# Three layers on one core: the experts' second product on 512 columns at once, and an output written in whole rows

## The chip, the core and the metric

The kernel runs on one core of one Trainium2 chip. The metric is the device time of one execution in microseconds (us), lower is better. Engines named here: PE (TensorE, matrix products), DVE (VectorE), ACT (ScalarE), POOL (GpSimd), and SP (SyncE), whose queue issues all transfers of this kernel. Matrix results land in PSUM, eight banks of 512 fp32 columns on 128 partitions; PSUM has to be copied to SBUF by DVE or ACT before a transfer can take it to HBM.

## What is computed

The reference chains three layers over 2304 tokens (4 batches of 576) of width 512: attention in a window (four heads) or a dilated window (four heads), a feed-forward layer `g = h - tanh(h)` with `h = x @ w_in` and `g @ w_out`, and a soft mixture of 8 experts with 4 slots each. The change lies at the end of the third:

```
logits = x @ phi                                   # 2304 x 32 slots
slot_input = softmax_over_tokens(logits).T @ x     # 32 x 512
for e in range(8):                                 # 4 slots each
    h = np.maximum(slot_input[e] @ w1[e], 0.0)     # 512 -> 1024
    slot_out[e] = h @ w2[e]                        # 1024 -> 512
c = softmax_over_slots(logits)                     # 2304 x 32
return c @ slot_out                                # 2304 x 512
```

## The kernel before

The program is written as one order of instructions per engine; nothing is reordered by a scheduler. Attention, the two weight matrices of the feed-forward layer, its tokens in chunks and the statistics of the logits fill the time up to about 440 us; there the slots' inputs are made. Nothing of this is touched.

Then follow the experts. Their weights are 32 tiles of 1 MB (`w1t`, `w2t`, two of each kind per expert, rows of 1024 fp32 in a tile), loaded by `load_experts` (L672, L676) into a ring of 21 equal buffers (`unit`) as these come free; in the trace they are named `ex`, their source `in_moe_w_dram`. `expert_up` makes the hidden layer of an expert, `expert_relu` turns it into columns in `hT`, which holds zeros but for the expert's own 4 of 32 slots, so that all experts can add into one result of 32 slots.

`expert_down(e, y, cols)` (L706 to L713) is the second product: 8 matmuls that take 32 columns of `hT` as weights and stream 256 columns of `w2t`. Four of them at a time stand on the four column strips of the PE array, so `y` has four partial sums on its 128 partitions. The columns are treated in two halves, each with its own PSUM tile (`ys`). The constant `DOWN` (L32) sets the order of experts and halves: experts 0 to 6 of half 0, experts 0 to 2 of half 1, expert 7 of half 0, the rest of half 1.

`combine(y, a)` is a generator that finishes half `a`: DVE copies `y` to SBUF (L1015); a product with `sum3` (L1018) adds the four strips and gives the result three times; ACT rounds it to a shorter fp32 form (L1019) and DVE puts the rounding error into the third copy (L1020), together `sS` (trace: `fin`); then nine pieces of output follow. Each is two matmuls `o` of 128 tokens by 256 columns (L1031) with the softmax weights `cT` or `cR`, one copy out of PSUM, by DVE for even pieces (L1038) and ACT for odd ones (L1036), and a write. A token's number is 4i + r in its batch; one tile `cT[:, b, r]` has 128 tokens of equal r. A piece holds r and r + 1 for 128 values of i, and its write (L1044) sends, for each token, 256 columns: 1 KB. The last piece holds the 64 left-over tokens of each batch and is written by four transfers of 64 KB (L1042). The pieces of half 0 are made two at a time between the experts of half 1.

Of the kernel before, what the change touches and what calls it, by code (L numbers as in the profile page):

```python
# [8 lines left out]
F32 = mybir.dt.float32  # L9
# [19 lines left out]
MASKPE = 2  # L29
PO = (2, 3, 0, 1)  # L30
ENGS = {'qk': 'AAAAVAAVVVAA', 'pt': 'AAA', 'hi': 'AAA', 'rem': 'VVA', 'wh': 'AV', 'wt': 'AA', 'wq': 'VA', 'wp': 'A', 'g': 'AAAA'}
DOWN = [(0, e) for e in range(7)] + [(1, e) for e in range(3)] + [(0, 7)] + [(1, e) for e in range(3, 8)]  # L32
WARM = 5
NWARM = 4
WAT = 0.29
# [25 lines left out]
def moe_kernel(ctx: ExitStack, tc: tile.TileContext, q, k, v, w_in, w_out, phi, w1, w2, out):  # L61
    nc = tc.nc
    B, H, S, D = q.shape
    DM, DFF = w_in.shape
    NS = phi.shape[1]
    NE, _, FE = w1.shape
# [8 lines left out]
    ps_h = ctx.enter_context(tc.tile_pool(name="ps_h", bufs=2, space=PSUM))  # L75
    ps_l = ctx.enter_context(tc.tile_pool(name="ps_l", bufs=1, space=PSUM))
    ps_m = ctx.enter_context(tc.tile_pool(name="ps_m", bufs=5, space=PSUM))

    def mm(shape):
        return ps_m.tile(shape, F32, tag="mm", name="mm")  # L80
# [15 lines left out]
    def copy(eng, out, in_):  # L96

        (nc.scalar.copy if eng == "A" else nc.vector.tensor_copy)(out=out, in_=in_)  # L98
# [7 lines left out]
    def unit(name, shape, dt=F32):  # L106
        return sb.tile(shape, dt, tag="unit", bufs=UNITS, name=name)

    def cpart(*dims):
        o = moff[0]  # L110
        moff[0] += size(dims)
        return view(mem[:, o:o + size(dims)], dims)

    class Ring:
# [5 lines left out]
        def next(self):  # L120
            self.n += 1
            return self.places[(self.n - 1) % len(self.places)]
# [30 lines left out]
    t_sb = cpart(512)  # L153
# [473 lines left out]
    halves = [slice(0, 256), slice(256, 512)]  # L627
# [19 lines left out]
    w1t, w2t, h1, hT = {}, {}, {}, []  # L647
# [55 lines left out]
            op0=ALU.max,  # L703
        )

    def expert_down(e, y, cols):  # L706
        for n in range(8):
            j, i = divmod(n, 2)
            qd = n % 4
            nc.tensor.matmul(  # L710
                y[32 * qd:32 * qd + 32, :], lhsT=hT[0][:, e, i, j, :], rhs=w2t[e, j // 2][:, j % 2, i, cols],
                start=(e == 0 and n < 4), stop=(e == NE - 1 and n >= 4), tile_position=(0, 32 * qd),
            )  # L713

# [57 lines left out]
    with tc.manual_schedule():  # L772
        conv_tiles()
        consts()
        steps = []
# [4 lines left out]
        for b, (t0, dt) in enumerate((ATT0, ATT1)):  # L780
            for i in range(NU):
                t = t0 + dt * i
# [16 lines left out]
        for e in range(NFT):  # L799
            t, dt = (WO1[0] + WO1[1] * e, WO1[1]) if e < KA else (WO2[0] + WO2[1] * (e - KA), WO2[1])  # L800
# [6 lines left out]
            t, dt = WI[0] + WI[1] * e, WI[1]  # L807
# [11 lines left out]
        for ft in range(NFT):  # L819
            t = HT[0] + HT[1] * ft  # L820
# [23 lines left out]
        for ch in range(1, 4):  # L844
            xh, xl = xhi[ch], xlo[ch]
            if ch == 3:
# [6 lines left out]
                t = unit("gr", [128, 3, 512])  # L853
# [4 lines left out]
            for s in range(NFT // 2):  # L858
                a, b = 2 * s, 2 * s + 1
# [40 lines left out]
        for s in range(NFT // 2):  # L900
            a = 2 * s
            ps = ps_h.tile([128, 512], F32, tag="h", name="h").rearrange("p (i t) -> p i t", i=2)
# [57 lines left out]
        for a, copy in enumerate((nc.scalar.copy, nc.vector.tensor_copy)):  # L960
            ps = mm([128, 2, 128])
# [7 lines left out]
        ps = mm([128, 512])  # L969
        for c in range(4):  # L970
            for fq in range(4):
                nc.tensor.matmul(
                    ps[32 * fq:32 * fq + 32, :], lhsT=tT[:, c, 32 * fq:32 * fq + 32], rhs=wo[fq][:, c, :],
                    start=(c == 0), stop=(c == 3), tile_position=(0, 32 * fq),
# [7 lines left out]
        for a, copy in enumerate((nc.scalar.copy, nc.vector.tensor_copy)):  # L982
            ps = mm([128, 2, 32])
# [20 lines left out]
        cT, cR, sS = fins  # L1004


        ov = out.rearrange("(b i r) d -> b i r d", b=B, r=4)
        ofl = out.rearrange("(b t) d -> b t d", b=B)
        sum3 = stack.rearrange("p j s -> p (j s)")[:, 0:96]

        def combine(y, a):

            cols = slice(256 * a, 256 * a + 256)
            ys = t_sb[:, cols]
            nc.vector.tensor_copy(out=ys, in_=y)  # L1015
            yield
            ps = mm([96, 256])
            nc.tensor.matmul(ps, lhsT=sum3, rhs=ys, start=True, stop=True)  # L1018
            nc.scalar.copy(out=sS[:, cols], in_=ps)  # L1019
            nc.vector.tensor_tensor(  # L1020
                out=sS[64:96, cols], in0=ps[64:96], in1=sS[64:96, cols].bitcast(F32), op=ALU.subtract
            )
            yield
            units = [(b, r) for b in range(B) for r in (0, 2)] + [(None, 0)]
            o = None
            for t, (b, r) in enumerate(units):
                pool = (ps_h, "h") if t % 3 == 0 else (ps_m, "mm")
                ps = pool[0].tile([128, 2, 256], F32, tag=pool[1], name="o")
                for x in range(2):
                    lhsT = cR[:, 2 * x:2 * x + 2].rearrange("p b i r -> p (b i r)") if b is None else cT[:, b, r + x]  # L1030
                    nc.tensor.matmul(ps[:, x], lhsT=lhsT, rhs=sS[:, cols], start=True, stop=True)  # L1031
                if t % 4 == 0:
                    o = unit("o", [128, 4, 2, 256])
                od = o[:, t % 4]
                if t % 2:
                    nc.scalar.copy(out=od, in_=ps)  # L1036
                else:
                    nc.vector.tensor_copy(out=od, in_=ps)  # L1038
                if b is None:
                    for n in range(B):  # L1040
                        x, h = divmod(n, 2)
                        nc.sync.dma_start(out=ofl[n, 512:576, cols], in_=od[64 * h:64 * h + 64, x])  # L1042
                else:
                    nc.sync.dma_start(out=ov[b, 0:128, r:r + 2, cols], in_=od)  # L1044
                yield


        ys = [ps_l.tile([128, 256], F32, tag="lg", name="y"), mm([128, 256])]
        halves2 = [combine(y, a) for a, y in enumerate(ys)]
        for a, e in DOWN:  # L1050
            expert_down(e, ys[a], halves[a])
            if a and DOWN.index((a, e)) > DOWN.index((0, NE - 1)):
                for _ in range(2):
                    next(halves2[0], None)
            if (a, e) == (0, NE - 1):
                next(halves2[0])
        for steps in halves2:
            for _ in steps:
                pass


# [28 lines left out]
```

## Time and profile before

| | before |
|---|---|
| time, median of 3 runs | 506.72 us (506.23 to 509.2) |
| the profiled execution | 506.77 us |
| its span, first to last instruction | 505.0 us |
| PE busy | 467.6 us, 93% of the span |
| DVE, ACT, POOL busy | 226.1, 233.6, 83.5 us |
| mean granted clock of PE | 0.973 of full |
| moved by DMA | 81.16 MB, 159 GB/s over the span |
| writes of the output | 16 of 256 KB and 8 of 64 KB |

The busy shares are means over stages with different limits, so they do not say what the last 40 us are bound by. The rows further down are read for that: the chain of waits tells which step the end hung on, a timeline tells what an engine did and what ended its idle time, and a table of stretches shows busy time, granted clock and DMA rate side by side. A group of matmuls in a timeline shows the time from the first start to the last end, with the drain of the last.

### The profile page before, as it was taken

To read this page: it belongs to the slowest core of one execution; us is meant where nothing else is said; L and a number is where in the kernel's file an instruction comes from. 1 tells how busy PE (TensorE), PEld (TensorE's weight loads), DVE (VectorE), ACT (ScalarE), POOL (GpSimd) and SP (SyncE) were. 2 spreads that over 40 slices of the span, in tenths; PEclk is the share of its full clock that TensorE was granted. 3 is DMA by queue.
4 is the path that set the end of the run, shared out by engine and by line. 5 is a ranking of instruction groups with operands and counts; after the bars stand their busy time and mean duration, and the time that the engine had idled before them with its cause. 6 is when DMAs were issued, how large, how long until landed. Compare 5 with 4: busy or idle time off the path is not lost.

```text
span 505.0 us, 11720 instructions
## 1 busy us (share of the span) xinstructions
PE 467.6 (93%) x4741; PEld 353.9 (70%) x4741; DVE 226.1 (45%) x560; ACT 233.6 (46%) x761; POOL 83.5 (17%) x99
## 2 busy tenths in 40 slices
PE   6879778999999999999999899999999999999872
PEld 5656556877777868888786778877677879645442
DVE  1669988945754435433242453432312231232032
ACT  3647636575655464675364556543223323213022
POOL 3263455432341010211011011100000000010000
PEclk9959988999999999999999999999999999999995
DMA  8989899644145602212310100219500279899946
GB/s 213 209 213 291 290 310 307 195 121 119 28 144 115 101 2 51 73 49 47 86 38 1 37 1 3 85 58 412 198 1 1 84 278 393 323 392 407 375 156 220
DMA packets 65029, 81.16 MB, mean 161 GB/s; under 512 B 35792, under 2 KB 44240, under 8 KB 64976
## 3 DMA queue, kind: packets, MB, share of 16 engines
q1 hardware_dynamic: 64976, 80.42, 50.8%
q8 instruction: 37, 0.61, 0.5%
q14 instruction: 16, 0.13, 0.1%
HBM read 71.50 MB, written 8.91 MB: 159 GB/s over the span
## 4 chain that ended last, share of the span: by engine, by line
PE 77%; DVE 8%; DMA 4%; ACT 4%; issue 4%; POOL 1%; SPq 0%; POOLq 0%; ACTq 0%; DVEq 0%
PE h L502 13%; PE h L503 12%; PE h L504 12%; PE mm L536 5%; PE mm L304 5%; PE lg L517 4%; PE mm L358 4%; DMA ex<-in_moe_w_dram 3%; PE mm L337 3%; PE mm L634 3%; PE mm L266 3%; PE h L685 2%; ACT mem L316 2%; DVE cva L442 1%; PE o L1031 1%
## 5 line engine op out<-in xcount | busy, mean ns | idle before, releaser
L502 PE MATMUL h<-xhi,whi 128*128 128x512 f32 x256 | 107.0, 418 | 0.0
L504 PE MATMUL h<-xhi,wlo 128*128 128x512 f32 x256 | 100.9, 394 | 0.0
L503 PE MATMUL h<-xlo,whi 128*128 128x512 f32 x256 | 100.8, 394 | 0.0
L508 ACT ACTIVATE mem<-h 128x512 f32<-128x512 f32 x56 | 33.4, 596 | 83.7 <-PE h L504 83.7
L511 DVE TENSOR_TENSOR mem<-h,mem 128x512 f32<-128x512 f32 x56 | 38.6, 689 | 73.1 <-ACT mem L508 72.8
L328 POOL TENSOR_TENSOR mem<-mem 128x320 f32<-128x320 f32 (+1 forms) x48 | 34.5, 718 | 188.5 <-DVE mem L327 126.0
L502 PEld LDWEIGHTS h<-xhi,whi 128*128 128x128 f32 x256 | 48.6, 190 | 13.2 <-issue 5.0
L504 PEld LDWEIGHTS h<-xhi,wlo 128*128 128x128 f32 x256 | 48.4, 189 | 10.8
L503 PEld LDWEIGHTS h<-xlo,whi 128*128 128x128 f32 x256 | 48.9, 191 | 8.9 <-DVE xlo L390 0.7
L98 ACT COPY g<-mm 128x512 f32<-128x512 f32 x72 | 40.2, 597 | 11.9 <-PE mm L549 4.8
L316 ACT ACTIVATE mem<-mm,mem 128x80 f32<-128x80 f32 (+1 forms) x84 | 26.8, 330 | 30.8 <-DVE mem L313 30.8
L316 ACT ACTIVATE mem<-mem 128x80 f32<-128x80 f32 (+1 forms) x84 | 29.9, 357 | 16.5 <-DVE mem L313 14.4
L304 PE MATMUL mm<-qk 64*64 64x96 f32 (+2 forms) x672 | 35.0, 250 | 1.9 <-DVE qk L98 1.9
L304 PEld LDWEIGHTS mm<-qk 64*64 64x64 f32 (+1 forms) x672 | 28.1, 135 | 10.2 <-issue 5.4
L337 PE MATMUL mm<-mem 112*80 112x112 f32 (+1 forms) x168 | 24.7, 274 | 10.3 <-POOL mem L328 7.7
L98 ACT COPY mem<-mm 80x448 f32<-80x448 f32 (+4 forms) x64 | 26.7, 441 | 13.3 <-DVE xlo L390 6.5
L310 DVE TENSOR_TENSOR mem<-mm,mem 128x320 f32<-128x320 f32 (+1 forms) x24 | 11.3, 470 | 42.1 <-PE mm L304 42.1
L511 DVE TENSOR_TENSOR gr<-h,gr 128x512 f32<-128x512 f32 x16 | 11.1, 692 | 42.2 <-ACT gr L508 42.2
L266 PE MATMUL mm<-mem,rqk 72*128 72x72 f32 x256 | 23.8, 240 | 5.0 <-POOL mem L160 3.4
L358 PEld LDWEIGHTS mm<-mem,v 80*64 80x64 f32 (+1 forms) x672 | 22.8, 139 | 7.1 <-issue 4.0
L536 PE MATMUL mm<-mem 128*128 128x128 f32 x192 | 27.6, 281 | 0.0
L358 PE MATMUL mm<-mem,v 80*64 80x48 f32 (+1 forms) x672 | 27.5, 228 | 0.0
(155 smaller groups left out, 749.1 us busy)
## 6 DMA issues: line engine op xcount, KB each, us to landing
ex<-in_moe_w_dram SPq DMA_DIRECT2D x30, 1024.0 KB
raww<-in_moe_w_out_dram SPq DMA_DIRECT2D x8, 1024.0 KB
raww<-in_moe_w_in_dram SPq DMA_DIRECT2D x8, 1024.0 KB
rqk<-in_k_dram SPq DMA_DIRECT2D x32, 144.0 KB
rqk<-in_q_dram SPq DMA_DIRECT2D x32, 144.0 KB
wo_dram<-cva SPq DMA_DIRECT2D x16, 256.0 KB
wo<-wo_dram SPq DMA_DIRECT2D x4, 1024.0 KB
out_dram<-o SPq DMA_DIRECT2D x16, 256.0 KB
```

Source lines behind the costliest of these rows:

```text
L98: (nc.scalar.copy if eng == "A" else nc.vector.tensor_copy)(out=out, in_=in_)
L266: nc.tensor.transpose(ps[:, r, :], raw[:, 4 * th + r], ident[0:72, 0:72])
L304: nc.tensor.matmul(ps[64 * x:64 * x + nr, c, :], lhsT=qT[b, p][r, q0:q0 + nr], rhs=kT[b, p][r, k0:k0 + nk], start=not by_pe, stop=True, sk ...
L316: nc.scalar.activation(out=pr[:, c, :], in_=ps[:, c, :], func=ACTF.Exp, bias=nm[:, c:c + 1], accum_out=sm[:, c:c + 1],)
L328: nc.gpsimd.tensor_tensor(out=pr, in0=pr, in1=rc.unsqueeze(2).to_broadcast([128, nb, nk]), op=ALU.mult)
L337: nc.tensor.transpose(ps[:, c, :], pr[0:P, c, :], ident[0:P, 0:P])
L358: nc.tensor.matmul(o[64 * hh:64 * hh + 64, col:col + nq], lhsT=vt[b, p](n, hh), rhs=pt[:, c, 64 * x:64 * x + nq], start=True, stop=True,)
L502: nc.tensor.matmul(ps, lhsT=wh, rhs=xh[:, kt, :], start=(kt == 0), stop=False)
L503: nc.tensor.matmul(ps, lhsT=wh, rhs=xl[:, kt, :], start=False, stop=False)
L504: nc.tensor.matmul(ps, lhsT=wl, rhs=xh[:, kt, :], start=False, stop=(kt == KT - 1))
L511: nc.vector.tensor_tensor(out=g, in0=ps, in1=g, op=ALU.subtract)
L536: nc.tensor.transpose(ps[:, j, :], g[:, 128 * j:128 * j + 128], ident)
```

## The change

`expert_down` loses its argument `cols` and streams all 512 columns into one PSUM tile `y`; `DOWN` goes, and experts 0 to 7 run one after another, two weight tiles each, in the order in which these are loaded. The generator goes too. `y` is copied to SBUF in two halves, by DVE and by ACT; the summing product and the rounding stay in two halves. Then the new helper `rows` makes 128 tokens by 512 columns with one matmul and copies them by DVE (even) or ACT (odd); two neighbouring r of one i lie next to each other in HBM, so a write sends 4 KB in one piece per partition, 512 KB in all; a left-over write has 2 KB pieces, 128 KB in all. Eight large and four small writes remain.

```
-DOWN = [(0, e) for e in range(7)] + [(1, e) for e in range(3)] + [(0, 7)] + [(1, e) for e in range(3, 8)]
...
-    def expert_down(e, y, cols):
+    def expert_down(e, y):
...
-                y[32 * qd:32 * qd + 32, :], lhsT=hT[0][:, e, i, j, :], rhs=w2t[e, j // 2][:, j % 2, i, cols],
+                y[32 * qd:32 * qd + 32, :], lhsT=hT[0][:, e, i, j, :], rhs=w2t[e, j // 2][:, j % 2, i, :],
...
-        def combine(y, a):
-
-            cols = slice(256 * a, 256 * a + 256)
-            ys = t_sb[:, cols]
-            nc.vector.tensor_copy(out=ys, in_=y)
-            yield
+        y = ps_l.tile([128, 512], F32, tag="lg", name="y")
+        for e in range(NE):
+            expert_down(e, y)
+        for cols, copy in zip(halves, (nc.vector.tensor_copy, nc.scalar.copy)):
+            copy(out=t_sb[:, cols], in_=y[:, cols])
+
+        for cols in halves:
             ps = mm([96, 256])
-            nc.tensor.matmul(ps, lhsT=sum3, rhs=ys, start=True, stop=True)
+            nc.tensor.matmul(ps, lhsT=sum3, rhs=t_sb[:, cols], start=True, stop=True)
...
+        def rows(t, lhsT, od):
+            pool = (ps_h, "h") if t % 3 == 0 else (ps_m, "mm")
+            ps = pool[0].tile([128, 512], F32, tag=pool[1], name="o")
+            nc.tensor.matmul(ps, lhsT=lhsT, rhs=sS, start=True, stop=True)
+            (nc.scalar.copy if t % 2 else nc.vector.tensor_copy)(out=od, in_=ps)
+
+        for b in range(B):
+            o = unit("o", [128, 4, 512])
+            for r in range(4):
+                rows(r, cT[:, b, r], o[:, r])
+                if r % 2:
+                    nc.sync.dma_start(out=ov[b, 0:128, r - 1:r + 1], in_=o[:, r - 1:r + 1])
+        o = unit("o", [128, 4, 512])
+        for x in range(2):
+            rows(x, cR[:, 2 * x:2 * x + 2].rearrange("p b i r -> p (b i r)"), o[:, x])
+            for h in range(2):
+                nc.sync.dma_start(out=ofl[2 * x + h, 512:576], in_=o[64 * h:64 * h + 64, x])
```

What each engine is given changes at the end alone. On PE, from the last transpose of `c` on, the order before is this (`y` is half 0, `mm` behind L710 half 1; the rest of the program is more `o` rows, another L1018 and the `o` rows of half 1):

```order
L938 MATMUL mm<-mem 96x128 x2
L710 MATMUL y<-ex,hT 32x256 x56
L710 MATMUL mm<-ex,hT 32x256 x24
L710 MATMUL y<-ex,hT 32x256 x8
L710 MATMUL mm<-ex,hT 32x256 x8
L1018 MATMUL mm<-mem 96x256
L1031 MATMUL o<-fin,cT 128x256 x2
L710 MATMUL mm<-ex,hT 32x256 x8
L1031 MATMUL o<-fin,cT 128x256 x4
L710 MATMUL mm<-ex,hT 32x256 x8
L1031 MATMUL o<-fin,cT 128x256 x4
```

Now it is this, to the end of the program:

```order
L699 MATMUL mm<-mem 128x128 x2
L937 MATMUL mm<-mem 96x128 x2
L709 MATMUL y<-ex,hT 32x512 x64
L1017 MATMUL mm<-mem 96x256 x2
L1026 MATMUL o<-fin,cT 128x512 x16
L1026 MATMUL o<-fin 128x512 x2
```

The 128 matmuls of 256 columns became 64 of 512, none of them stands behind or between output matmuls any more, and 36 output matmuls of 256 columns became 18 of 512.

On SP, the last transfers before (`ex` are the last weight tiles):

```order
L676 DMA ex<-in_moe_w_dram 128x2x1024 x16
L1044 DMA out_dram<-o 128x2x256 x8
L1042 DMA out_dram<-o 64x256 x4
L1044 DMA out_dram<-o 128x2x256 x8
L1042 DMA out_dram<-o 64x256 x4
```

and now:

```order
L655 DMA wo<-wo_dram 128x4x512 x4
L671 DMA ex<-in_moe_w_dram 128x2x1024 x7
L675 DMA ex<-in_moe_w_dram 128x2x1024 x16
L1034 DMA out_dram<-o 128x1024 x8
L1039 DMA out_dram<-o 64x512 x4
```

The two rounds of writes became one, with two tokens of 512 columns in a row of 1024. On ACT, with the semaphores that each instruction waits for, the end of the program now begins so (L1013 is the copy of the second half of `y`, L1018 the rounding, L1027 the output's copies):

```order
L943 CAST fin<-mm 96x3x16
L1013 COPY mem<-y 128x256 [waits DVE_49]
L1018 CAST fin<-mm 96x256 [waits PE_49] x2
L1027 COPY o<-o 128x512 [waits DMAHW2_49,PE_49]
L1027 COPY o<-o 128x512 [waits PE_49]
```

The ACT copy of `y` waits for DVE, whose copy of the other half of the same PSUM tile stands ahead of it; before, ACT had no part in copying `y`.

## Rows read from the trace of the kernel before

**Rows 1.** Chain that ended last, from 440 us: start, us, what
```profile
463.02 17.41 DMA ex<-in_moe_w_dram
...
496.63 0.69 DVE o L1038
```

**Rows 2.** Timeline of PE from 467.5: start, us, engine, line, op, tiles, count [idle before]
```profile
467.92 5.82 PE L710 MATMUL y<-ex,hT 128*32 128x256 f32 x104
...
475.37 0.64 PE L710 MATMUL y<-ex,hT 128*32 128x256 f32 x8 [1.64 <-DMA ex<-in_moe_w_dram]
...
480.47 0.64 PE L710 MATMUL y<-ex,hT 128*32 128x256 f32 x8 [1.44 <-DMA ex<-in_moe_w_dram]
...
483.49 0.51 PE L1031 MATMUL o<-fin,cT 96*128 96x256 f32 x2 [0.92 <-DVE fin L1020]
...
490.27 0.40 PE L1031 MATMUL o<-fin 96*128 96x256 f32 x2
...
493.43 2.73 PE L1031 MATMUL o<-fin,cT 96*128 96x256 f32 x16 [0.92 <-DVE fin L1020]
...
495.96 0.63 PE L1031 MATMUL o<-fin 96*128 96x256 f32 x2
```

**Rows 3.** Stretches: from:to, us, busy of five engines, PEclk, DMA share, GB/s
```profile
485.50:487.00 1.50, 1.50 (x21) 0.83 (x20) 0.69 (x1) 0.55 (x1) 0.00 (x0) 1.00 0.50 178
487.00:493.00 6.00, 4.31 (x45) 2.27 (x44) 2.46 (x5) 2.12 (x4) 0.00 (x0) 1.00 0.93 312
493.00:495.50 2.50, 2.07 (x14) 2.08 (x15) 1.91 (x4) 1.23 (x3) 0.00 (x0) 0.85 0.35 87
495.50:501.75 6.25, 1.09 (x6) 0.79 (x4) 1.66 (x3) 1.02 (x2) 0.00 (x0) 0.50 1.00 334
501.75:503.75 2.00, 0.00 (x0) 0.00 (x0) 0.00 (x0) 0.00 (x0) 0.00 (x0) 0.50 0.50 136
```

**Rows 4.** Timeline of SP, the writes of the output
```profile
484.75 6.70 SPq L1044 DMA_DIRECT2D out_dram<-o  x8
...
499.79 2.66 SPq L1042 DMA_DIRECT2D out_dram<-o  x4
```

**Rows 5.** Timeline of PE from 443.0 and from 445: L972, clipped to each window
```profile
442.79 3.19 PE L972 MATMUL mm<-wo,mem 128*32 128x512 f32 x28
...
444.51 1.47 PE L972 MATMUL mm<-wo,mem 128*32 128x512 f32 x12
```

**Rows 6.** Timeline of all engines from 445: operations behind the second product
```profile
481.18 0.43 DVE L1015 COPY mem<-y 128x256 f32<-128x256 f32 x1 [12.60 <-PE y L710]
...
484.03 0.69 DVE L1038 COPY o<-o 128x512 f32<-128x512 f32 x1 [0.60 <-PE o L1031]
...
485.47 0.58 ACT L1036 COPY o<-o 128x512 f32<-128x512 f32 x1 [2.49 <-PE o L1031]
...
491.31 0.41 DVE L1015 COPY mem<-mm 128x256 f32<-128x256 f32 x1
...
491.87 0.64 PE L1018 MATMUL mm<-mem 128*96 128x256 f32 x2 [1.21 <-DVE mem L1015]
...
492.55 0.37 ACT L1019 CAST fin<-mm 96x256 fp32r<-96x256 f32 x1 [1.50 <-PE mm L1018]
...
492.95 0.42 DVE L1020 TENSOR_TENSOR fin<-mm,fin 32x256 fp32r<-32x256 f32 x1 [1.23 <-ACT fin L1019]
```

**Rows 7.** Stretches, columns as in Rows 3: two of weight loads, one write of `wo_dram`
```profile
450.00:452.00 2.00, 2.00 (x34) 1.10 (x30) 1.20 (x4) 0.53 (x2) 0.76 (x1) 1.00 1.03 420
...
456.00:458.00 2.00, 2.00 (x38) 1.23 (x34) 0.48 (x2) 0.77 (x3) 0.00 (x0) 1.00 1.01 401
...
93.50:93.75 0.25, 0.25 (x8) 0.18 (x10) 0.25 (x1) 0.00 (x0) 0.00 (x0) 1.00 0.98 385
```

**Rows 8.** Stretches of 0.25 us at the first and the last written data
```profile
485.50:485.75 0.25, 0.25 (x6) 0.16 (x8) 0.05 (x1) 0.25 (x1) 0.00 (x0) 1.00 0.29 106
...
503.50:503.75 0.25, 0.00 (x0) 0.00 (x0) 0.00 (x0) 0.00 (x0) 0.00 (x0) 0.50 0.02 4
```

More of the change, by code (lines that the diff above doesn't have):

```diff
@@ L1022, in combine @@
             )
[L1023 to L1045, printed above, removed]
@@ L1048, in moe_kernel @@
[L1048 to L1059, printed above, removed]
+        def rows(t, lhsT, od):
[3 more added lines that the diff above has]
+            (nc.scalar.copy if t % 2 else nc.vector.tensor_copy)(out=od, in_=ps)
```

## The prediction

> **What bounds the kernel now.** I read the chain of work that ended last first, from 440 us on, because everything in the diff comes after that. In it one step is a load: `ex`, a weight tile of the experts, holds the chain for 17.41 us, and the chain's last engine step is a copy of an output tile by VectorE (DVE) [rows 1]. So near the end the kernel goes from waiting for weights to making and writing output. The timeline of TensorE (PE) shows the hand-over: the second product (L710) starts at 467.92, runs 104 instructions without a stop, stands 1.64 us and later 1.44 us for `ex`, and takes its last 8 instructions for columns 0 to 255 at 480.47, when the last tile has landed [rows 2]. An fp32 matmul is two instructions in the trace, so 64 matmuls (all experts, 256 columns) are 128 instructions.
>
> The second reading is the table of stretches behind 485 us [rows 3]. The DMA engines are the work there: busy 0.93 to 1.00 in 487 to 493 and in 495.5 to 501.75, but only 0.35 in 493 to 495.5, where the second half of the columns is still being made, and 0.50 at the start and in the last two microseconds. PE, DVE and ACT have nothing left in that last stretch. Third, the queue that issues the writes (SP): the first write goes at 484.75; the last four, of 64 KB each, are issued one after another over 2.66 us from 499.79 [rows 4], with the engines half idle beside them. The end is thus: product, a short serial chain, then 4.72 MB of output (16 x 256 KB and 8 x 64 KB) through DMA engines that are fed with gaps.
>
> **Step 1: the product, on 512 columns.** The change takes away the order that ran columns 0 to 255 first, and issues 128 instructions of 512 columns. Their price stands in the trace, in another product of the same form (128x32 weights, 512 columns, four column strips at a time, L972): 28 instructions take 3.19 us and the last 12 of them 1.47, so 16 take 1.72, or 0.43 us for four, and the last four need 0.61 until their end (1.47 less 2 x 0.43) [rows 5]. From 467.92, 31 x 0.43 to the start of the last four, and 0.61 more: 481.86. The tile that lands at 480.47 is used by the last eight, which start at 467.92 + 30 x 0.43 = 480.82. PE no longer waits for weights; it is itself the bound, by 0.35 us. Now columns 0 to 255 are ready at 480.47 + 0.64 = 481.11 [rows 2]. So this step costs **+0.75 us**.
>
> **Step 2: from the product to the first write.** Rows for every operation exist [rows 6]. DVE begins 0.07 us behind the product's end and copies 256 columns in 0.43: 482.36. The ACT copy of the other half reads the same tile and waits for DVE in the order; 0.37 us, by the ACT row of nearly the same size: 482.75. It is hidden by the first sum (L1018 now), which PE starts 0.15 behind the DVE copy (491.31 + 0.41 to 491.87) and ends 0.64 later: 483.15. The second sum follows after two more passes of about 0.22 us (256 columns each, half of the 0.43): 483.61. Each half then takes ACT 0.37 and DVE 0.42, with 0.03 to 0.04 us between: DVE ends the first at 484.01 and the second at 484.47. PE starts the output 0.06 later (492.95 + 0.42 to 493.43 [rows 2]); 512 columns cost 0.51, as two matmuls of 256 do now [rows 2]: 485.04. DVE copies in 0.69, to 485.77; ACT, one matmul (0.23) later, in 0.58, to 485.89. A write now needs both, and is issued at 485.92, where the first one now goes at 484.75. That is **+1.17 us** with step 1 in it. The copies lose nothing after that: two tiles (512 KB) in each 0.69 us on two engines, against 1.28 us that writing 512 KB will need (below). Should PE's clock have fallen to 1.2 GHz by then, as it has behind 495.5 [rows 3], a pair of matmuls costs about 0.86 us, still under 1.28, and only the first pair comes some 0.35 us later. It fell there after pauses like those of this chain, so I keep 0.35 as a bound.
>
> **Step 3: the writes.** From the first issue (484.75) to the first moved data it is 0.93 us: the window from 485.50 has a share of 0.29, so data runs from 485.68 [rows 8]. After: from 486.85. What does a 4 KB piece cost on the way out? No write of that size is in the trace, so I bound it. Below: the output's own 1 KB pieces move at 334 GB/s over 6.25 us [rows 3]. Above: the loads of weights, whose pieces are 4 KB, move at 401 to 420 GB/s [rows 7]. Between them lies a write: `wo_dram`, 2 KB pieces, alone on the engines, at 385 GB/s [rows 7]. That is where it would lie if the piece's size counts and the direction does not, so I take the loads' middle, 410, for 4 KB. The 8 large writes (4.19 MB): 10.23 us, or 1.28 each. The 4 small ones have 2 KB pieces (0.52 MB at 385): 1.36. Sum 11.59, without a gap, since SP issues all 12 by about 494 while data runs to 498.44. From the last data (503.5 [rows 8]) to the end of the span it is 1.5 us now, and stays: 499.94. The stretch from first to last data shrinks from 17.8 to 11.6 us, **-6.2 us**: about 3.8 are the gaps of [rows 3] (0.75 + 0.4 + 1.6 + 1.0), the rest the piece size.
>
> The Trainium skill ("DMA: Bandwidth & Descriptors", Where 436 GB/s comes from) speaks against the second part: for transfers between HBM and SBUF the HBM side binds, at about 358 GB/s per core. By that rule 1 KB pieces are nearly at the limit already, the output takes 13.2 us instead of 11.59, and the sum would be 503.3. This trace does not agree as far as it goes, with 401 to 420 for loads over microseconds and 385 for a write [rows 7]; but that write is one of 256 KB, and no row shows a long one.
>
> **Other edits.** Nothing ahead of 467.92 moves in the order on any engine. The five output buffers (six before) take the places of expert tiles read long before. SP has 12 issues in place of 24; all but the first lie beside running data. Their cost would come back if the queue ran empty (second rival).
>
> **Sum.** Span 505.0 + 1.17 - 6.23 = 499.94. The profiled execution took 506.77, 1.77 more than its span; the median shown is 506.72, so the two agree. **501.7 us**.
>
> **Rivals.**
> - *The rate does not rise with the piece, or not all the way.* For it: the steady 334 GB/s, and that no long write with larger pieces is in the trace. Against: [rows 7]. Price: 4.72 MB at 334 are 14.1 us, 2.5 more: 504.2; at 372, half-way to 410, 12.7 us: 502.8. Chance 0.18.
> - *The last writes are limited by their issue again.* For it: now 2.66 us for four, at a DMA share of 0.50. If SP is held up so long that the queue runs empty ahead of the last four, the 1.0 us of that gap returns: 502.7. Against: their data is ready near 491.5, with some seven microseconds of writes ahead of them. Chance 0.10.
> - *Slower: PE's clock falls in the product.* PE now is the bound there, so its clock is on the path. At 1.2 GHz four instructions cost 0.86; the two levels show in two small matmuls, 0.63 at 495.96 against 0.40 at 490.27 [rows 2]. All 32 fours would cost 13.8 us more: 515. It decides from 12 fours on (5.06 / 0.43): beyond that the kernel is slower than before. Against: the granted clock is 1.00 on both sides of the product [rows 3, 7], though PE pauses in it for 1.64 and 1.44 us [rows 2], and these pauses go. Chance 0.03.
>
> **How the numbers follow.** The forecast, 501.1 to 502.5 (rate 420 or 401, with or without the 0.35 us), has 0.64; 0.05 lies under it. A change of 1%, about what a measurement of this kernel can tell from none, ends at 501.65, in the middle of the forecast, and since the 0.35 us can only add, I put 0.35 of the 0.64 below it: with the 0.05, faster 0.40. Same: the other 0.29, with 0.18 and 0.10: 0.57. Slower 0.03. The range takes in the issue rival and most of the rate rival: 501.0 to 503.8.
>
> **What the next profile would show.** Step 1: L709 from 467.9 to 481.9 without idle time for `ex`. Step 2: the first write at 485.9. Step 3: a DMA share near 1.00 and 400 GB/s or more from 487 to 498, no dip, a short tail. At 335 to 375 GB/s the rate rival is right; a share falling to half near the end is the issue rival; a granted clock under 1.00 ahead of 481 the third. A first write behind 486.5 would break step 2, and an `ex` wait behind 480.8 step 1.

## The result, and the profile after

The changed kernel took 503.41 us (median of 20 runs), the kernel before, on the same chip, 508.21 us (20 runs): a ratio of 0.991, with a 95% interval of 0.9883 to 0.9937. On 508.21 that is 4.6 us less (3.2 to 5.9); the forecast was 5.06 less, a ratio of 0.990. The time came out 1.7 us above the forecast of 501.7: inside the range of 501.0 to 503.8, but above the narrower 501.1 to 502.5. Most of the 1.7 us is the start of the sum, for the kernel before measured 1.5 us more in this comparison than the median from which the sum was made. The ratios here and below leave out executions more than 1.5% above the fastest of their kernel; the profiles of e2, e4 and e5 are of such executions.

The profiled execution of the changed kernel took 504.57 us with a span of 502.8 us. The chain of work that ended last, from 440 us (start, us, what), answers to [rows 1]:

```profile
464.90 18.11 DMA ex<-in_moe_w_dram
483.01 0.04 issue
483.06 1.11 PE y L709 x8
...
492.60 0.58 ACT o L1027
```

It still hangs on a weight tile. The timeline of all engines from 465 us (start, us, engine, line, op, tiles, count, idle time before and its releaser) answers to [rows 2, 4, 6]:

```profile
469.80 13.08 PE L709 MATMUL y<-ex,hT 128*32 128x512 f32 x120
...
483.06 1.06 PE L709 MATMUL y<-ex,hT 128*32 128x512 f32 x8 [0.17 <-DMA ex<-in_moe_w_dram]
484.19 0.43 DVE L1013 COPY mem<-y 128x256 f32<-128x256 f32 x1 [13.74 <-PE y L709]
...
484.67 1.11 PE L1017 MATMUL mm<-mem 128*96 128x256 f32 x4 [0.55 <-DVE mem L1013]
485.38 0.80 ACT L1018 CAST fin<-mm 96x256 fp32r<-96x256 f32 x2 [0.36 <-PE mm L1017]
485.78 0.85 DVE L1019 TENSOR_TENSOR fin<-mm,fin 32x256 fp32r<-32x256 f32 x2 [1.17 <-ACT fin L1018]
...
486.69 5.05 PE L1026 MATMUL o<-fin,cT 96*128 96x512 f32 x16 [0.91 <-DVE fin L1019]
...
488.07 7.92 SPq L1034 DMA_DIRECT2D out_dram<-o  x8
...
496.08 3.86 SPq L1039 DMA_DIRECT2D out_dram<-o  x4
```

The product runs 120 instructions without a stop where it stood 1.64 and 1.44 us before, and waits 0.17 us ahead of its last eight. The serial chain follows in the order of the prediction, and the first write is issued at 488.07. The stretches from there (from:to, us, busy time of PE, weight loads, DVE, ACT and POOL, granted clock of PE, DMA share, GB/s) answer to [rows 3, 8]:

```profile
488.00:489.00 1.00, 1.00 (x4) 0.65 (x4) 1.00 (x2) 0.79 (x3) 0.00 (x0) 1.00 0.09 37
489.00:499.00 10.00, 3.30 (x11) 1.64 (x10) 4.06 (x7) 3.56 (x7) 0.00 (x0) 0.88 1.02 406
499.00:500.00 1.00, 0.00 (x0) 0.00 (x0) 0.00 (x0) 0.00 (x0) 0.00 (x0) 0.50 0.93 242
500.00:501.00 1.00, 0.00 (x0) 0.00 (x0) 0.00 (x0) 0.00 (x0) 0.00 (x0) 0.50 0.92 326
501.00:501.75 0.75, 0.00 (x0) 0.00 (x0) 0.00 (x0) 0.00 (x0) 0.00 (x0) 0.50 0.28 79
```

Ten microseconds at 406 GB/s stand where [rows 3] has 312, 87 and 334. Then comes a stretch that the forecast did not have: at 499 the engines are still busy (0.93) but move only 242 GB/s, and at 501 the share is 0.28. Most of these 2.75 us belong to the four writes of left-over tokens: without them (e6 below) the data of the large writes last 10.52 us, and 10.52 us from the first data here (488.94) end at 499.46.

**How the runs are compared below.** The product began at 467.92 us before and at 469.80 now, although nothing ahead of it moved; over all profiled executions of this study it began between 465.90 and 474.81 us. That variation is larger than any term in dispute. So everything below is counted from the first instruction of the second product to the end of the span, which holds all that the change touches. Each row of the table is one profiled execution, and not all are of one chip. How far its hundredths can be trusted is seen from the two profiles of the changed kernel, whose output data last 12.57 us both times, though the last weight tile came 0.63 us later in one of them. In us behind that instruction:

| kernel | last weight tile in | product ends | first write issued | output data, first to last (length) | end of span |
|---|---|---|---|---|---|
| before | 12.51 | | 16.83 | 17.73 to 35.64 (17.91) | 37.04 |
| forecast | 12.55 | 13.94 | 18.00 | 18.93 to 30.52 (11.59) | 32.02 |
| changed | 13.21 | 14.32 | 18.27 | 19.14 to 31.71 (12.57) | 33.00 |
| changed, second profile | 12.58 | 13.94 | 17.90 | 18.76 to 31.33 (12.57) | 32.62 |
| e1: pieces of 1 KB | 12.51 | 13.94 | 17.34 | 18.24 to 34.26 (16.02) | 35.66 |
| e2: pieces of 2 KB | 12.55 | 13.94 | 17.76 | 18.62 to 31.84 (13.22) | 33.14 |
| e3: left-over second | 12.56 | 13.94 | 17.90 | 18.76 to 31.34 (12.58) | 32.64 |
| e4: left-over on ACT's queue | 14.41 | 15.52 | 20.61 | 21.48 to 35.56 (14.08) | 36.79 |
| e5: left-over spread | 12.95 | 14.06 | 18.01 | 18.87 to 31.01 (12.14) | 32.32 |
| e6: no left-over writes | 12.60 | 13.94 | 17.90 | 18.76 to 29.28 (10.52) | 30.67 |
| e7: spread, ahead of the last batch | 12.42 | 13.94 | 17.89 | 18.75 to 31.11 (12.36) | 32.42 |
| e8: two merged writes, batch outermost | 12.65 | 13.94 | 17.90 | 18.76 to 41.26 (22.50) | 42.49 |
| e9: two merged writes, token outermost | 12.46 | 13.94 | 17.89 | 18.75 to 30.60 (11.85) | 31.85 |

From before to the second profile: first write +1.07, length of the data −5.34, the rest (issue to data, tail) −0.15, in all −4.42 us. That agrees with the 4.6 us of the timed runs.

### The profile page after: what moved, and what is told of

Same layout as the page of the kernel before. It is cut to its first block, busy times and chain, and to the rows that moved or that the text cites. A ratio compares the mean times of both kernels' runs of the same rounds, so it can differ in the third digit from the quotient of the medians.

```text
span 502.8 us, 11407 instructions
## 1 busy us (share of the span) xinstructions
PE 468.3 (93%) x4595; PEld 350.3 (70%) x4595; DVE 224.6 (45%) x558; ACT 234.4 (47%) x763; POOL 83.9 (17%) x99
## 4 chain that ended last, share of the span: by engine, by line
PE 77%; DVE 7%; DMA 5%; ACT 4%; issue 4%; POOL 1%; SPq 0%; POOLq 0%; ACTq 0%; DVEq 0%
PE h L501 13%; PE h L503 13%; PE h L502 12%; PE mm L303 6%; PE mm L535 5%; PE lg L516 4%; PE mm L357 4%; DMA ex<-in_moe_w_dram 4%; PE mm L336 3%; PE mm L633 3%; PE mm L265 3%; PE h L684 2%; ACT mem L315 2%; DVE cva L441 1%; PE mm L466 1%
```

## Experiments

**The changed kernel once more**, unedited, for the size of what varies.

> The changed kernel once more, unedited. Its profiled execution had the last weight tile 13.2 us behind the product's first instruction, four other executions 12.5. Theory (0.35 to 0.40 us of its 33.0 are that late tile, and the product is otherwise bound by TensorE as forecast): with a tile at 12.5 the product takes 13.9, the first write goes at 17.9, the end comes at 32.5 to 32.7 us. Rival (the product waits for weights whenever it is not interleaved): 14.3 and 33.0 again with a tile at 12.5.

503.71 us (6 runs), a ratio of 0.9904 (0.9867 to 0.9941). In its timeline PE does not stop at all:

```profile
468.74 13.94 PE L709 MATMUL y<-ex,hT 128*32 128x512 f32 x128
```

So the wait of 0.17 us and the late first write of the first profile are not the rule: in eight of the eleven profiled executions with the new product the last tile is in by 12.42 to 12.65, and the product takes 13.94.

**e1: the product on 512 columns alone, the output as before.** Two rounds of 256 columns, 1 KB pieces, 24 writes, all behind the product.

```
-        for b in range(B):
-            o = unit("o", [128, 4, 512])
...
+        for cols in halves:
...
+                    for n in range(B):
+                        x, h = divmod(n, 2)
+                        nc.sync.dma_start(out=ofl[n, 512:576, cols], in_=od[64 * h:64 * h + 64, x])
+                else:
+                    nc.sync.dma_start(out=ov[b, 0:128, r:r + 2, cols], in_=od)
```

> The new product on 512 columns, but output made and written as before: 256 columns at a time, 1 KB pieces, 24 writes, all behind the product. Measured from the first instruction of the second product to the end of the span, where the kernel before takes 37.1 us and the changed one 33.0. Theory (the gain has two parts, the closed gap and the larger piece): product 14.2, first write at about 17.6, 13.8 us of data without a gap, a tail limited by the issue of the last four writes: 34.5 to 35.0. Rival (the piece size alone gives the gain, and the later start of the writes costs what the closed gap brings): 36.5 to 37.2.

35.66, a ratio of 0.996 (0.9918 to 1.0003): between the two expectations. Making all the output in one go closes less than expected. The stretches say why (columns as above):

```profile
491.00:495.00 4.00, 2.90 (x21) 2.34 (x19) 4.00 (x8) 2.95 (x6) 0.00 (x0) 1.00 1.00 335
...
497.00:498.00 1.00, 0.00 (x0) 0.00 (x0) 0.00 (x0) 0.00 (x0) 0.00 (x0) 0.55 0.72 213
498.00:499.00 1.00, 0.00 (x0) 0.00 (x0) 0.00 (x0) 0.00 (x0) 0.00 (x0) 0.50 0.51 123
499.00:500.00 1.00, 0.00 (x0) 0.00 (x0) 0.00 (x0) 0.00 (x0) 0.00 (x0) 0.50 0.89 298
500.00:504.00 4.00, 0.00 (x0) 0.00 (x0) 0.00 (x0) 0.00 (x0) 0.00 (x0) 0.50 1.02 341
...
506.00:507.00 1.00, 0.00 (x0) 0.00 (x0) 0.00 (x0) 0.00 (x0) 0.00 (x0) 0.50 0.51 126
```

The compute engines are done by 495.5 us, and still the DMA share drops to 0.51 in the middle. SP's timeline shows what is issued there:

```profile
495.26 2.66 SPq L1042 DMA_DIRECT2D out_dram<-o  x4
```

Four writes of 64 KB over 2.66 us feed the engines no more than 0.26 MB / 2.66 us = 99 GB/s. The kernel before had four such writes in the middle as well:

```profile
491.54 2.48 SPq L1042 DMA_DIRECT2D out_dram<-o  x4
```

Its hole at 493 to 495.5, a share of 0.35 [rows 3], looked like output that was not made yet; a hole of 0.72 and 0.51 over two microseconds is here too, with all output made.

**e2: pieces of 2 KB.** Each tile of 128 tokens is written by itself, 16 writes of 256 KB instead of 8 of 512 KB.

```
-                if r % 2:
-                    nc.sync.dma_start(out=ov[b, 0:128, r - 1:r + 1], in_=o[:, r - 1:r + 1])
+                nc.sync.dma_start(out=ov[b, 0:128, r], in_=o[:, r])
```

> The changed kernel with one write for each 128 tokens (2 KB pieces, 256 KB, 16 writes and the four small ones). Theory (the rate goes by the piece, 385 GB/s at 2 KB against 405 at 4 KB): 0.6 us more data time, the first write about 0.1 us earlier: 33.4 to 33.7 us from the product's first instruction to the end. Rival (2 KB is as good as 4 KB, and the neighbouring tokens bring nothing): 32.8 to 33.1.

33.14, a ratio of 0.9893 (0.9823 to 0.9963), just above the lower of the two expectations. Both ranges were set against the first profile (33.00); against the second (32.62) they would lie 0.38 lower, and 33.14 would be in that of the theory. Against the second profile of the changed kernel the data take 0.65 us longer and the first write goes 0.14 earlier. The steady stretch:

```profile
494.25:503.75 9.50, 2.76 (x10) 1.32 (x8) 3.42 (x6) 2.94 (x6) 0.00 (x0) 0.70 1.05 377
```

With e1 this gives the rate by piece, all writes, over microseconds: 335 to 341 GB/s at 1 KB, 377 at 2 KB, 406 at 4 KB. A longer piece does pay, and more than half of the rise is there at 2 KB.

**e3: the left-over writes moved up**, behind the first batch, so that their issue lies beside running data.

```
+        def rest():
...
+            if b == 0:
+                rest()
```

> The changed kernel with the left-over tokens (four writes of 128 KB) made and written behind the first batch in place of last. Theory (the last 2.5 us are limited by issuing these four writes behind a full queue, each held until earlier ones land): the end is a 512 KB write whose data follow without a pause: 32.1 to 32.4 us from the product's first instruction to the end. Rival (the end is limited by the DMA engines and the time to land, wherever the small writes stand): 32.8 to 33.1.

32.64, a ratio of 0.9901 (0.9859 to 0.9943): between the two ranges, and the same as the second profile without the move (32.62). Lowered by the same 0.38, the range of the rival holds it. Stretches around the left-over writes and behind them:

```profile
488.75:491.25 2.50, 1.38 (x5) 0.67 (x4) 2.09 (x4) 1.89 (x4) 0.00 (x0) 1.00 0.91 287
491.25:498.75 7.50, 0.00 (x0) 0.00 (x0) 0.00 (x0) 0.00 (x0) 0.00 (x0) 0.51 1.02 405
```

The slow stretch moves with the writes: their cost is their own, not that of standing last.

**e4: the left-over writes from ACT's queue**, so that two queues issue.

```
-                nc.sync.dma_start(out=ofl[2 * x + h, 512:576], in_=o[64 * h:64 * h + 64, x])
+                nc.scalar.dma_start(out=ofl[2 * x + h, 512:576], in_=o[64 * h:64 * h + 64, x])
```

> The changed kernel with the four small writes issued from the queue of ACT in place of SP; order and place of everything else unchanged. Theory (SP's queue is held up, each issue until an earlier write has landed, and the small ones come late for that): issued at about 493 from ACT, they move beside the large ones, 32.1 to 32.5 us from the product's first instruction to the end. Rival (what holds up the issue is shared by the queues, or it's the engines): 32.8 to 33.2.

504.48 us, a ratio of 0.9942 (0.9899 to 0.9985): no gain that the timed runs show, and the stretch of 36.79 us cannot be compared, for a weight tile came in only at 14.41. ACT's first issue takes 0.54 us, the other three 1.38 to 1.87, so in this execution the second queue did not get past the hold that SP's issues meet. The late tile is of use for something else; this is what it did, in the timeline of PE:

```profile
488.00 1.06 PE L709 MATMUL y<-ex,hT 128*32 128x512 f32 x8 [1.37 <-DMA ex<-in_moe_w_dram]
489.62 1.76 PE L1017 MATMUL mm<-mem 128*96 128x256 f32 x4 [0.55 <-DVE mem L1013]
```

and in one stretch:

```profile
491.00:494.25 3.25, 2.33 (x6) 1.53 (x6) 1.77 (x4) 0.95 (x2) 0.00 (x0) 0.50 0.00 0
```

PE stood 1.37 us for the tile and 0.55 for the copy of `y`. The granted clock then falls in the sums (0.73 over 489 to 491) and is at half (1.2 GHz) for the rest of the chain; the sums take 1.76 us instead of 1.11, and from the product's end to the first write it is 5.09 us instead of 3.96.

**e5: the left-over tokens spread over the partitions.** The 64 tokens of a write stood on partitions 0 to 63 or 64 to 127; here two batches alternate, so that each write reads every second partition of 128. The rows of `cR` are put in that order where they are made; what else is computed is the same (`rest` is a flat view of them).

```
-            rows(x, cR[:, 2 * x:2 * x + 2].rearrange("p b i r -> p (b i r)"), o[:, x])
+            rows(x, rest[:, 128 * x:128 * x + 128], o[:, x])
...
-                nc.sync.dma_start(out=ofl[2 * x + h, 512:576], in_=o[64 * h:64 * h + 64, x])
+                nc.sync.dma_start(out=ofl[2 * x + h, 512:576], in_=o[h:128:2, x])
```

> The changed kernel with the left-over tokens of two batches on alternate partitions: each of the four small writes reads 64 partitions spread over all 128, in place of 64 neighbouring ones. Sizes, order, queue and place stay. Theory (a write from 64 neighbouring partitions moves at about half the rate, which the forecast left out; the four cost 2.3 us of data time in place of 1.36): 31.5 to 31.9 us from the product's first instruction to the end. Rival (these writes are slow because each is issued late behind a full queue): 32.4 to 32.7.

32.32, between the two; with the first write 0.11 late for its weights, 32.2. The data take 12.14 us, 0.43 less than in the second profile; the timed ratio, 0.9917 (0.9881 to 0.9953), cannot show so little. Stretches at the end, which answer to 499 to 501.75 of the changed kernel:

```profile
503.25:504.25 1.00, 0.00 (x0) 0.00 (x0) 0.00 (x0) 0.00 (x0) 0.00 (x0) 0.50 0.97 373
504.25:505.25 1.00, 0.00 (x0) 0.00 (x0) 0.00 (x0) 0.00 (x0) 0.00 (x0) 0.50 0.65 250
```

The stretch of busy engines at 242 GB/s is gone (0.97 and 373 GB/s, the rate of 2 KB pieces), and of the 2 KB packets, whose median is 84 ns in both kernels, the slowest twentieth took over 200 ns in the changed kernel and over 86 ns now. The Trainium skill ("SBUF — State Buffer", Door 1: The DMA port swizzle) says that partitions 0 to 63 reach only 8 of the 16 ports of SBUF, and 64 to 127 the other 8. The trace agrees in kind: 242 GB/s in the stretch with 64 neighbouring partitions, 373 in that with 64 alternate ones, both with the end of the large writes in them. The low rate is not there all the time, as two half microseconds of the changed kernel show:

```profile
499.50:500.00 0.50, 0.00 (x0) 0.00 (x0) 0.00 (x0) 0.00 (x0) 0.00 (x0) 0.50 0.96 201
500.00:500.50 0.50, 0.00 (x0) 0.00 (x0) 0.00 (x0) 0.00 (x0) 0.00 (x0) 0.50 1.04 389
```

Why the second is fast was not tried; two writes from different halves of the partitions can be under way together there. What is left in e5 is a share of 0.65. Within it the share falls to 0.26 from 504.50 to 504.75 and comes back to 0.68: engines that have nothing to move between two writes.

**e6: no left-over writes.** They are left out, so 256 of the 2304 tokens are not written.

```
-            for h in range(2):
-                nc.sync.dma_start(out=ofl[2 * x + h, 512:576], in_=o[64 * h:64 * h + 64, x])
```

> The changed kernel without the four small writes: the left-over 256 tokens are computed and copied, but not written. The difference to the whole kernel is their price at the end. Theory (half rate or late issue): 2.2 us or more, so the end at 30.2 to 30.4 us with a tile at 12.5. The forecast's own price, 1.36 us: the end at 31.2 to 31.3.

30.67 (one execution), nearer to the theory than to the forecast's price. The eight large writes take 10.52 us, and so the four small ones cost 12.57 − 10.52 = 2.05 us of data, where the forecast had 1.36.

**e7: spread, and ahead of the last batch**, with the edits of e5.

```
+        def left():
...
+            if b == B - 1:
+                left()
```

> Alternate partitions as in the run before, and the left-over tokens made and written behind the third batch in place of last, so that a full queue stands ahead of them and large writes behind them. Theory (only the rate of the small writes matters): as with alternate partitions alone, 31.5 to 31.9. Theory (late issue costs something too, since the last two small writes come behind 1 us of blocked issue): 0.2 to 0.4 less than that one.

32.42, a ratio of 0.9922 (0.9888 to 0.9956): above both expectations and no better than e5; the data take 0.22 us longer than there. Two stretches:

```profile
493.25:494.25 1.00, 0.00 (x0) 0.00 (x0) 0.00 (x0) 0.00 (x0) 0.00 (x0) 0.50 0.59 223
494.25:496.75 2.50, 0.00 (x0) 0.00 (x0) 0.00 (x0) 0.00 (x0) 0.00 (x0) 0.50 1.01 408
```

The engines run empty (0.59) in the middle, with all data made. SP's issues are held 1.1 to 1.3 us each from the fourth to the eighth, the first two small ones among them; the last two small ones take 0.55 and 0.59 us, and at 128 KB each that feeds the engines some 230 GB/s. SP is then only about three writes ahead, here as at the end of the order.

**e8: two merged writes.** If it is the number of issues, two batches in one write of 256 KB should end it.

```
-            for h in range(2):
-                nc.sync.dma_start(out=ofl[2 * x + h, 512:576], in_=o[64 * h:64 * h + 64, x])
+            nc.sync.dma_start(out=ofl[2 * x:2 * x + 2, 512:576], in_=o[:, x])
```

> All times from the first instruction of the second product to the end of the span, as in the other runs. The four left-over writes of 128 KB (64 neighbouring partitions each) become two of 256 KB, 128 partitions each, last in the order as in the changed kernel; nothing else is touched. Known: without left-over writes 30.67 us; with them from 64 neighbouring partitions 32.62; with them spread over all partitions, still four issues, 32.32. Theory (of the 1.95 us that the left-over output costs, 0.3 is the slow rate out of 64 neighbouring partitions and 0.3 a queue that runs dry since four issues of 0.55 to 0.60 us each stand behind a held one): two issues and 128 partitions take both away; 0.52 MB at about 400 GB/s are 1.3 us, so 31.9 to 32.0, without a stretch below a share of 0.9 until the last half microsecond. Rival (the spread alone was all there is to gain; the rest is what 2 KB pieces and a write's own tail cost): 32.2 to 32.4, as with the spread.

42.49, and a ratio of 1.009 (1.0054 to 1.0126): 10 us longer than the changed kernel, neither theory. Stretches:

```profile
490.75:500.75 10.00, 3.23 (x11) 1.64 (x10) 3.98 (x7) 3.48 (x7) 0.00 (x0) 0.72 1.02 405
...
505.00:513.00 8.00, 0.00 (x0) 0.00 (x0) 0.00 (x0) 0.00 (x0) 0.00 (x0) 0.50 0.13 51
```

The large writes are as ever; then the DMA share stands at 0.13, as much as two of sixteen engines at work. The write's destination is 2 batches by 64 tokens by 512 columns, with the 2 outermost. Two engines that move 256 pieces of 84 ns need 10.8 us, most of the tail of 12. The count of packets under 512 B says the same, first for the second profile of the changed kernel, then for e8 (from 485 us):

```profile
DMA packets 1472, 4.72 MB, mean 157 GB/s; under 512 B 192, under 2 KB 192, under 8 KB 1472
...
DMA packets 1412, 4.72 MB, mean 157 GB/s; under 512 B 132, under 2 KB 132, under 8 KB 1412
```

These small packets, of 4 bytes, come with the writes: 192 are 16 for each of twelve, and 132 are 16 for each of the eight large writes and 2 for each of the two merged ones. The Trainium skill ("DMA: Bandwidth & Descriptors", Why a DMA increments its semaphore by 16 and not by 1) states the rule that both expectations missed: a transfer uses the largest number of engines up to 16 that divides the slowest dimension of both sides. The trace agrees: 2 of 16.

**e9: two merged writes with the token outermost**, on the spread tokens of e5, so that the destination is 64 by 2 by 512.

```
-            for h in range(2):
-                nc.sync.dma_start(out=ofl[2 * x + h, 512:576], in_=o[h:128:2, x])
+            nc.sync.dma_start(out=ofl[2 * x:2 * x + 2, 512:576].rearrange("h t d -> t h d"), in_=o[:, x])
```

> The left-over tokens of two batches alternate on the partitions (token t of batch h at partition 2t + h), so that one write of 256 KB takes both with the token as its outer dimension (64 x 2 x 512 elements), where the merged write before had the batch outermost (2 x 64 x 512). Times from the first instruction of the second product to the end of the span. Theory (a write is handed to the DMA engines by its outer dimension: 2 occupied two of sixteen engines at a share of 0.12 to 0.13, 64 will occupy all): the tail at two engines goes; 8 large writes end 10.5 us behind the first data, 0.52 MB at about 400 GB/s add 1.3: 31.9 to 32.0, against 32.62 for the changed kernel and 42.49 with the batch outermost. Rival 1 (a merged write of 256 KB with 2 KB pieces at the queue's end is slow whatever its order of dimensions): 36 or more. Rival 2 (only the spread over the partitions counts, two issues fewer give nothing): 32.2 to 32.4.

31.85, a ratio of 0.9898 (0.9866 to 0.993). The stretches:

```profile
487.00:497.50 10.50, 3.55 (x12) 1.66 (x11) 4.30 (x7) 3.78 (x7) 0.00 (x0) 0.73 1.00 399
497.50:498.50 1.00, 0.00 (x0) 0.00 (x0) 0.00 (x0) 0.00 (x0) 0.00 (x0) 0.50 0.97 377
498.50:499.25 0.75, 0.00 (x0) 0.00 (x0) 0.00 (x0) 0.00 (x0) 0.00 (x0) 0.50 0.51 202
```

This is what the theory asked for, a little under its range and far from both rivals: the left-over output costs 11.85 − 10.52 = 1.33 us, the 1.36 of the forecast, and the stretch is 0.77 us shorter than that of the changed kernel. By the trace it is shorter than both kernels; the timed runs tell it from the kernel before, and not from the changed one (0.9898 against 0.991 and 0.9904).

## Why the prediction was right, and where its sum was off

The size was right: 5.06 us less forecast, 4.6 (3.2 to 5.9) timed, 4.42 by the trace. So was the path, a longer product paid back by output in fewer, longer pieces; why the DMA engines had gaps was read wrongly in part. The outcome, under 1%, is what the prediction called the same and gave 0.57. There is luck in it: 5.06 us of 506.72 is 0.999%, so the forecast lay on the border of the two outcomes, as the prediction says. The forecast's bounds are not those of its terms: 420 and 401 GB/s for the large writes, with or without the 0.35 us, give about 501.5 to 502.3 and not 501.1 to 502.5. Step by step, in the frame of the table:

**Step 1, the product.** Forecast 13.94 us, PE the bound by 0.35. Measured 13.94 in eight of eleven executions, by the price of another product [rows 5]. The margin against the weights is as thin as it was worked out, and in the other three the last tile was late (12.95, 13.21, 14.41; the product then ended at 14.06, 14.32 and 15.52). The sign set for this, a wait for `ex`, is there in the first profile; it is worth 0.38 us in it. Two stretches of that profile show the tile's last data coming in:

```profile
480.00:482.00 2.00, 2.00 (x24) 0.65 (x20) 0.00 (x0) 0.00 (x0) 0.00 (x0) 1.00 0.57 229
482.00:483.00 1.00, 0.88 (x12) 0.00 (x0) 0.00 (x0) 0.00 (x0) 0.00 (x0) 1.00 0.11 41
```

The share of 0.11 is the end of the tile on a few of the sixteen engines: four packets are in flight at 482.0 us, and the last ends at 482.56. The kernel before had a trailing end too, a share of 0.24 from 479 to 480. What made it later here was not tried and stays open.

**Step 2, to the first write.** Forecast 18.00, measured 17.90. The chain of seven operations was priced from [rows 6] and holds. The bound for a fallen clock, 0.35 us, was too small: it counted the first pair of output matmuls and left out the sums ahead of it. e4, the one execution with a fallen clock there, shows 1.13 us (5.09 against 3.96).

**Step 3, the writes.** This is the term that was off: 11.59 us forecast, 12.57 measured, and two parts make the 0.98. The eight large writes took 10.52 (e6) where 10.23 was forecast, +0.29: 4.19 MB in 10.52 us are 399 GB/s over the whole with its edges, against the 410 assumed. The left-over writes took 2.05 in place of 1.36, +0.69. They were priced by their bytes, at a rate taken from a write of 128 partitions [rows 7], and neither assumption held: 64 neighbouring partitions go out slowly (0.43 us, e5), and four issues, of which the last two come 0.6 us apart, leave the engines without work for a while (0.29 us, by two larger writes in their place, e5 to e9). With both taken away (e9) the price of the forecast is met.

The sentence that failed is "SP issues all 12 by about 494". SP's last four writes were issued from 496.08 to 499.94. SP spends about 0.4 us on each of its first three writes, and from the fourth to the tenth 1.12 to 1.32 us each, about as long as the data of one large write take (1.28 forecast). So it runs only some three writes ahead, and the cover that the forecast gave to the small issues ran out: the last of them was issued from 499.34, when the large writes' data were all but out.

The cause of the gaps was wrong too, in a way that the sum hid. Forecast: 3.8 us from the gaps, 2.4 from the piece size. The second holds, as an estimate: 4.72 MB take 14.0 us at 338 GB/s, the middle of e1's stretches, and 11.6 at 406. But output made in one go (e1) closes only 17.91 − 16.02 = 1.89 of the gaps, since these were in part the small writes themselves, which stay. Pieces of 2 KB with half as many small writes give 2.80 (16.02 to 13.22), piece size and gap together, and 4 KB another 0.65.

**The tail** took 1.29 us instead of 1.5, and issue to data 0.86 instead of 0.93. So the sum for the second profile: −0.10 − 0.07 + 0.98 − 0.21 = +0.60 on 32.02, which is 32.62.

**The rivals.** *The rate does not rise*: refuted, 406 GB/s over 10 us. Its milder form had priced the output at 12.7 us, and 12.57 came; the length alone would have spoken for it, and only the stretches show that the large writes ran near the full rate (406 GB/s) and that most of the loss lay in the small ones. With it falls, for this kernel on one core, what the Trainium skill says in "DMA: Bandwidth & Descriptors", Where 436 GB/s comes from: a bound of about 358 GB/s per core between HBM and SBUF. The trace does not agree, for loads (401 to 420 [rows 7]) or for writes (406). *The last writes limited by their issue*: right in kind, and its sign, a share that falls to half near the end, is there (0.28 from 501.0); it costs 0.29 us instead of the 1.0 it was priced at. *PE's clock*: it did not fall in the product; the granted clock is 1.00 there in all eleven profiles.

## What to carry to other kernels

Price a write by three things besides its bytes: the time to issue it (here at the least 0.54 us for 128 KB from 64 partitions, more than the 0.36 for 512 KB from 128), the partitions that it reads, and the outermost dimension of its destination. The left-over end of a tensor can fail on all three. A gap with idle compute engines ahead of it can be the queue that issues and not the data: look at what stands in that queue beside the gap before calling it late output. Where the runs vary by more than the term in dispute, compare a stretch of the trace that starts at one instruction and holds all that was changed.

## What was not expected of the hardware

- A write of 256 KB whose destination had 2 as its outermost dimension ran on two of sixteen DMA engines, 51 GB/s (e8); the same bytes with 64 outermost, on alternating partitions, ran at 377 (e9).
- In the microsecond in which they set in, writes of 64 neighbouring partitions moved 242 GB/s at a DMA share of 0.93; of 64 alternate ones 373 at 0.97 (e5). A high share is not a high rate.
- SP's issues were held from the fourth write of 512 KB on, with 256 KB (e1) from the fifth, and ACT's beside them from its second (e4). What holds them was not tried.
- A write of 64 partitions took longer to issue than a larger one of 128: 0.57 us as SP's third (e3) against 0.36 to 0.40 for the first three of the changed kernel.
- With the same program ahead of it, the product began between 468.02 and 474.81 us in the profiles of the new product (465.90 in e7, whose edit also reorders some copies ahead of it); two unedited executions lay 1.06 us apart there (469.80 and 468.74).
